# Group normalisation in a ring of six slots: VectorE's loop rewritten with fixed addresses

## Chip, cores and metric

One core of one Trainium2 chip. The metric is the device time of one execution in microseconds (us), median of several runs. The kernel before takes 631.02 us (six runs, 630.43 to 631.61).

## The reference, cut to what matters

```python
# x: [128, 1024, 32, 16] bf16, 32 groups of 32 channels; g, b: [1024] bf16
xr  = x.reshape(B, G, C // G, H, W)
mu  = xr.mean(axis=(2, 3, 4), keepdims=True)
var = ((xr - mu) ** 2).mean(axis=(2, 3, 4), keepdims=True)
xn  = (xr - mu) / jnp.sqrt(var + 1e-5)
return xn.reshape(B, C, H, W) * g[None, :, None, None] + b[None, :, None, None]
```

Every element is read once and written once: 134.22 MB in and 134.22 MB out.

## The kernel before

The 128 images are cut into 32 tiles of 4 images x 32 groups = 128 partitions, each with 16384 elements (4.19 MB). A ring in SBUF has six slots of one tile. For a tile, TensorE adds 12 chunks of 512 columns in PSUM and VectorE adds the rest ("the pair"); ScalarE turns that into the mean, takes the sum of squares in two passes and the standard deviation; VectorE makes scale and bias and applies them in place, one channel (512 columns) per instruction, 32 per tile. Every tile is loaded and stored by one transfer, except that the last one is stored in four parts.

```python
SLOTS = 6
RUNS = (2, 3, 3, 3, 3, 3, 3, 3, 3, 6)       # stores in a row, then as many loads
...
def on_sync(e):                              # issues all transfers, in one queue
    def load(j):
        if j >= SLOTS:
            e.wait_ge(st[j % SLOTS], 16 * (j // SLOTS))       # the slot's store has landed
        e.dma_start(out=slot(j), in_=x_v[j]).then_inc(ld[j % SLOTS], 16)
    def store(i): ...                        # waits for done (VectorE's apply), then dma_start
    for j in range(1, SLOTS):
        load(j)
    i = 0
    for run in RUNS:
        for n in range(run):
            store(i + n)
        i += run
        for j in range(i + SLOTS - run, min(i + SLOTS, NT)):
            load(j)
...
def on_vector(e):
    bytes_of_ring = ring[:].bitcast(mybir.dt.uint8)
    def part(i, lo, n):                      # address from the loop's register
        at = (i % SLOTS) * (F * ITEM) + lo * ITEM
        return bytes_of_ring[:, bass.ds(at, n * ITEM)].bitcast(BF16)
    def pair(i):
        e.wait_ge(first_in, i + 1)           # TensorE's first chunk of this tile
        e.scalar_tensor_tensor(out=jp[:], in0=part(i, lo, n), ..., accum_out=ps[...]).then_inc(paired, 1)
    pair(0)
    with nc.Fori(0, NT, 1, engines=[e.engine]) as i:          # one tile per trip
        with e.If(i < NT - 1):
            e.drain()
            pair(i + 1)
        parts = [part(i, k * HW, HW) for k in range(KC)]
        e.wait_ge(stded, i + 1)
        e.reciprocal(out=rstd[:], in_=std[:, bass.ds(i % SLOTS, 1)]).then_inc(inverted, 1)
        ...                                  # scl, then bia, each after a wait on the one before
        for k, a in enumerate(parts):        # the apply
            ts = e.tensor_scalar(out=a, in0=a, scalar1=scl[:, k : k + 1], scalar2=bia[:, k : k + 1], ...)
            if (k + 1) % KQ == 0:
                ts.then_inc(done, 1)
```

TensorE and ScalarE already loop over six slots with fixed addresses (`in_rounds`: six rounds, of which the last has two tiles).

## Time and profile before

| | before |
|---|---|
| time, median of six | 631.02 us |
| span of the profiled run | 629.3 us |
| busy: VectorE (DVE), ScalarE (ACT), TensorE (PE) | 84%, 80%, 25% |
| mean rate of the transfers | 427 GB/s, in most slices 433 |
| mean granted TensorE clock | 0.595 |

A busy share is an average over stages, so 84% for VectorE says neither that it bounds the kernel nor that it doesn't.

### The profile page before, as it was taken

The page shows a single profiled execution, that of the slowest core. Times are in us where ns is not written, and L with a number is a line of the kernel's source. Part 1 is how long each engine was busy: PE and PEld are TensorE (multiplying, and loading weights), DVE is VectorE, ACT ScalarE, POOL GpSimd, SP SyncE. Part 2 cuts the span into 40 slices and gives each one's busy share as a digit, 9 for nine tenths or more (in the row PEclk, how much of TensorE's full clock was granted, in tenths as well). Part 3 has the DMA queues.
Part 4 walks back from the last instruction along what each step waited for, and adds up shares of the span by engine and source line. Part 5 has one row for each costly group of instructions (what it writes and reads, how often), then busy time and mean ns, then how long its engine had stood idle before and what let it go on. Part 6 is the DMA issues. An engine that isn't in the chain of part 4 may idle for free.

```text
span 629.3 us, 2573 instructions
## 1 busy us (share of the span) xinstructions
PE 157.9 (25%) x380; PEld 0.2 (0%) x2; DVE 529.7 (84%) x1185; ACT 504.0 (80%) x258; POOL 1.0 (0%) x8
## 2 busy tenths in 40 slices
PE   2433333222222220332063014203220430052000
PEld 0000000000000000000000000000000000000000
DVE  1579999999999999699689959995998699599963
ACT  0798999999999999699948977894999489859960
POOL 0000000000000000000000000000000000000000
PEclk9756655566666665566566557656665665576555
DMA  9999999999999999999999999999999999999996
GB/s 400 433 433 402 433 433 433 433 433 431 431 433 433 433 433 433 433 429 433 433 433 431 431 433 431 433 433 433 429 433 433 433 429 433 433 429 431 433 423 271
DMA packets 9744, 268.44 MB, mean 427 GB/s; under 512 B 1168, under 2 KB 1168, under 8 KB 1168
## 3 DMA queue, kind: packets, MB, share of 16 engines
q1 hardware_dynamic: 9648, 268.44, 99.3%
q10 hardware_dynamic: 96, 0.00, 0.0%
HBM read 134.22 MB, written 134.22 MB: 427 GB/s over the span
## 4 chain that ended last, share of the span: by engine, by line
DMA 49%; ACT 35%; DVE 7%; issue 4%; DVEq 2%; PE 2%; SPq 0%; ACTq 0%
DMA out_dram<-ring 33%; ACT ja L259 32%; DMA ring<-in_x_dram 14%; DVE ring L322 6%; DMA gb_b<-in_b_dram 2%; PE ps L213 2%; ACT jm L251 1%; DVEq L305 1%; ACT var L269 1%; ACT std L273 1%; DVE jp L289 0%; DVEq L308 0%; DVE bia L316 0%; DVE scl L312 0%; SPq L158 0%
## 5 line engine op out<-in xcount | busy, mean ns | idle before, releaser
L259 ACT ACTIVATE ja<-ring,nm 128x8192 fp8e5<-128x8192 bf16 x64 | 455.8, 7122 | 2.1
L322 DVE TENSOR_SCALAR ring<-ring,scl,bia x1024 | 333.7, 410 | 1.2
L213 PE MATMUL ps<-ring,eye 128*128 128x512 bf16 x379 | 157.7, 588 | 421.6 <-DVE jp L289 292.3
L289 DVE SCALAR_TENSOR_TENSOR jp<-ring 128x5120 fp8e5 (+1 forms) x32 | 175.8, 5493 | 58.3 <-PE ps L213 46.3
L251 ACT ACTIVATE jm<-ps 128x513 fp8e5<-128x513 f32 x32 | 19.2, 601 | 97.8 <-PE ps L213 97.8
L310 DVE RECIPROCAL rstd<-std 128x1 f32 x32 | 6.3, 198 | 12.1 <-ACT std L273 12.1
L259 ACT ACTIVATION_READ_ACCUMULATOR ja<-ring,nm 128x1 f32 x64 | 11.9, 186 | 0.0
L316 DVE SCALAR_TENSOR_TENSOR bia<-scl,nm,gb 128x32 f32<-128x32 f32 x32 | 8.0, 251 | 4.2
L301 DVE COPY gb<-gb_p 128x64 f32<-128x64 f32 x1 | 0.2, 225 | 12.6 <-PE gb_p L208 12.6
L273 ACT ACTIVATE std<-sq,var 128x1 f32<-128x1 f32 x32 | 9.4, 294 | 1.0
L269 ACT ACTIVATE var<-sq,eps_t 128x1 f32<-128x1 f32 x32 | 9.4, 294 | 1.0
L312 DVE TENSOR_SCALAR scl<-gb,rstd 128x32 f32<-128x32 f32 x32 | 7.7, 241 | 1.1
L251 ACT ACTIVATION_READ_ACCUMULATOR jm<-ps 128x1 f32 x32 | 6.2, 194 | 0.0
L289 DVE DVE_READ_ACCUMULATOR jp<-ring (+1 forms) x32 | 4.5, 142 | 0.0
L208 PE MATMUL gb_p<-gb_b,rep 32*128 32x64 bf16 x1 | 0.2, 206 | 12.4 <-DMA gb_b<-in_b_dram 12.4
L247 ACT ACT_TABLE_LOAD x1 | 1.3, 1283 | 1.8 <-issue 1.8
L190 POOL TENSOR_SCALAR_AFFINE_SELECT rep<-ones_b 32x128 bf16<-32x128 bf16 x1 | 0.3, 302 | 0.0
L186 POOL TENSOR_SCALAR_AFFINE_SELECT eye<-ones_b 128x128 bf16<-128x128 bf16 x1 | 0.3, 292 | 0.4 <-issue 0.4
L247 ACT ACTIVATE warm<-eps_t 128x1 f32<-128x1 f32 x1 | 0.2, 203 | 0.0
L180 POOL MEMSET ones_b<- 128x128 bf16 x1 | 0.2, 204 | 0.3 <-POOLq L355 0.3
L210 PEld LDWEIGHTS <-eye 128*128 128x128 bf16 x1 | 0.1, 106 | 0.1
L208 PEld LDWEIGHTS gb_p<-gb_b,rep 32*128 32x128 bf16 x1 | 0.1, 100 | 12.3 <-issue 12.3
(5 smaller groups left out, 0.5 us busy)
## 6 DMA issues: line engine op xcount, KB each, us to landing
ring<-in_x_dram SPq DMA_DIRECT2D x32, 4096.0 KB, 29.2
out_dram<-ring SPq DMA_DIRECT2D x31, 4096.0 KB, 31.6
out_dram<-ring SPq DMA_DIRECT2D x4, 1024.0 KB, 6.9
gb_b<-in_g_dram ACTq DMA_DIRECT2D x1, 2.0 KB, 7.8
gb_b<-in_b_dram ACTq DMA_DIRECT2D x1, 2.0 KB, 11.0
```

The lines of the kernel that those rows point to most:

```text
L213: return e.add_instruction(mybir.InstMatmult(name=nc.get_next_instruction_name(), engine=e.engine, start_tensor_calc=(k == 0), stop_tensor ...
L247: e.activation(out=warm[:], in_=eps_t[:], func=ACT.Sqrt)
L251: e.activation(out=jm[:], in_=sums_and_pairs(c), func=ACT.Identity, scale=-inv_n, accum_out=nm[:, c : c + 1], saturate=False,).then_inc(me ...
L259: e.activation(out=ja[:], in_=slot(c)[:, h * (F // 2) : (h + 1) * (F // 2)], func=ACT.Square, bias=nm[:, c : c + 1], scale=1.0, accum_out= ...
L269: e.activation(out=var[:], in_=sq[:, 0:1], func=ACT.Identity, bias=eps_t[:], scale=inv_n).then_inc(varred[c], 1)
L273: e.activation(out=std[:, c : c + 1], in_=sq[:, 1:2], func=ACT.Sqrt, bias=var[:], scale=inv_n).then_inc(stded, 1)
L289: e.scalar_tensor_tensor(out=jp[:], in0=part(i, lo, n), scalar=1.0, in1=part(i, lo + n, n), op0=ALU.mult, op1=ALU.add, accum_out=ps[:, bas ...
L305: e.drain()
L310: e.reciprocal(out=rstd[:], in_=std[:, bass.ds(i % SLOTS, 1)]).then_inc(inverted, 1)
L312: e.tensor_scalar(out=scl[:], in0=gb[:, 0:KC], scalar1=rstd[:], scalar2=None, op0=ALU.mult).then_inc(scaled, 1)
L316: e.scalar_tensor_tensor(out=bia[:], in0=scl[:], scalar=nm[:, bass.ds(i % SLOTS, 1)], in1=gb[:, KC : 2 * KC], op0=ALU.mult, op1=ALU.add,). ...
L322: ts = e.tensor_scalar(out=a, in0=a, scalar1=scl[:, k : k + 1], scalar2=bia[:, k : k + 1], op0=ALU.mult, op1=ALU.add,)
```

## The change

VectorE gets the six-slot loop of the other engines. The intent: addresses known when the program is built, no register arithmetic, no drain, semaphores per slot, and less time of VectorE between instructions. A pair now waits for the load itself. Its code becomes some six times as long.

```diff
-            e.wait_ge(first_in, i + 1)
+            e.wait_ge(ld[c], turn * 16)
             e.scalar_tensor_tensor(
                 out=jp[:],
-                in0=part(i, lo, n),
+                in0=slot(c)[:, first : first + w],
 ...
-        with nc.Fori(0, NT, 1, engines=[e.engine]) as i:
-            with e.If(i < NT - 1):
-                e.drain()
-                pair(i + 1)
-            parts = [part(i, k * HW, HW) for k in range(KC)]
-            e.keepalive_nop([e.lower_ap(a) for a in parts])
-            e.wait_ge(stded, i + 1)
-            e.reciprocal(out=rstd[:], in_=std[:, bass.ds(i % SLOTS, 1)]).then_inc(inverted, 1)
+        def one(c, t):
+            then = (c + 1) % SLOTS, t + (1 + (c + 1) // SLOTS)
+            if c == REST - 1:
+                with e.If(t < ROUNDS - 1):
+                    pair(*then)
+            else:
+                pair(*then)
+            e.wait_ge(stded[c], t + 1)
+            e.reciprocal(out=rstd[:], in_=std[:, c : c + 1]).then_inc(inverted[c], 1)
 ...
-            for k, a in enumerate(parts):
+            for k in range(KC):
+                a = slot(c)[:, k * HW : (k + 1) * HW]
 ...
+        pair(0, 1)
+        e.wait_ge(paired[0], 1)
+        in_rounds(e, one)
```

Cut: the semaphores that become one per slot (`paired`, `stded`, `inverted`, `scaled`, `shifted`), TensorE's last chunk waiting on `paired[c]`, and a count of store parts in the load's wait that changes no value here. RUNS and the 12 chunks stay as they were.

More of the change, by code (lines that the diff above doesn't have):

```diff
@@ L128, in sems @@
         return [sem(f"{name}{c}") for c in range(SLOTS)]
-    ld, st, summed, meaned = (sems(n) for n in ("ld", "st", "sum", "mean"))
-    half, both, varred = (sems(n) for n in ("half", "both", "var"))
-    inverted, scaled, shifted = (sem(n) for n in ("inv", "scl", "bia"))
-    first_in, paired, stded, done = (sem(n) for n in ("first", "pair", "std", "done"))
-    s_gb, s_ones, s_eye, s_gbp, s_fin = (
-        sem(n) for n in ("gbl", "ones", "eye", "gbp", "fin")
-    )
+    ld, st, summed, paired, meaned, stded = (
+        sems(n) for n in ("ld", "st", "sum", "pair", "mean", "std")
+    )
+    half, both, varred, inverted, scaled, shifted = (
+        sems(n) for n in ("half", "both", "var", "inv", "scl", "bia")
+    )
+    done = sem("done")
+    s_gb, s_ones, s_eye, s_gbp, s_fin = (sem(n) for n in ("gbl", "ones", "eye", "gbp", "fin"))
     def store_parts(i):
@@ L156, in load @@
             if j >= SLOTS:
-                e.wait_ge(st[j % SLOTS], 16 * (j // SLOTS))
+                e.wait_ge(
+                    st[j % SLOTS], 16 * sum(store_parts(i) for i in range(j % SLOTS, j, SLOTS))
+                )
             e.dma_start(out=slot(j), in_=x_v[j]).then_inc(ld[j % SLOTS], 16)
@@ L234, in one @@
                 elif k == PE_CHUNKS - 1:
-                    e.wait_ge(paired, t * SLOTS + (c + 1))
+                    e.wait_ge(paired[c], t + 1)
                 mm = add_up(sums(c), slot(c)[:, k * MM_FREE : (k + 1) * MM_FREE], k)
-                if k == 0:
-                    mm.then_inc(first_in, 1)
             mm.then_inc(summed[c], 1)
@@ L254, in one @@
             ).then_inc(meaned[c], 1)
-            for h, (ready, at) in enumerate(
-                ((meaned[c], t + (2 if c >= SLOTS - 2 else 1)), (half[c], t + 1))
-            ):
-                e.wait_ge(ready, at)
+            e.wait_ge(meaned[c], t + (2 if c >= SLOTS - 2 else 1))
+            for h in range(2):
+                if h == 1:
+                    e.wait_ge(half[c], t + 1)
                 e.activation(
@@ L266, in one @@
                     saturate=False,
-                ).then_inc((half, both)[h][c], 1)
+                ).then_inc(both[c] if h == 1 else half[c], 1)
             e.wait_ge(both[c], t + 1)
@@ L274, in one @@
                 out=std[:, c : c + 1], in_=sq[:, 1:2], func=ACT.Sqrt, bias=var[:], scale=inv_n
-            ).then_inc(stded, 1)
+            ).then_inc(stded[c], 1)
         in_rounds(e, one)
     def on_vector(e):
-        bytes_of_ring = ring[:].bitcast(mybir.dt.uint8)
-        def part(i, lo, n):
-            at = (i % SLOTS) * (F * ITEM) + lo * ITEM
-            return bytes_of_ring[:, bass.ds(at, n * ITEM)].bitcast(BF16)
-        def pair(i):
-            lo, n = PE_CHUNKS * MM_FREE, PAIRED // 2
-            e.wait_ge(first_in, i + 1)
+        e.wait_ge(s_gbp, 1)
@@ L289, in pair @@
+        e.tensor_copy(out=gb[:], in_=gb_p[:])
+        def pair(c, turn):
+            first, w = PE_CHUNKS * MM_FREE, PAIRED // 2
+            e.wait_ge(ld[c], turn * 16)
             e.scalar_tensor_tensor(
                 out=jp[:],
-                in0=part(i, lo, n),
+                in0=slot(c)[:, first : first + w],
                 scalar=1.0,
-                in1=part(i, lo + n, n),
+                in1=slot(c)[:, first + w : first + 2 * w],
                 op0=ALU.mult,
                 op1=ALU.add,
-                accum_out=ps[:, bass.ds((i % PS_BUFS) * (2 * MM_FREE) + MM_FREE, 1)],
+                accum_out=ps[:, c % PS_BUFS * 2 * MM_FREE + MM_FREE :][:, 0:1],
@@ L297, in pair @@
                 saturate=False,
-            ).then_inc(paired, 1)
-        e.wait_ge(s_gbp, 1)
-        e.tensor_copy(out=gb[:], in_=gb_p[:])
-        pair(0)
-        with nc.Fori(0, NT, 1, engines=[e.engine]) as i:
-            with e.If(i < NT - 1):
-                e.drain()
-                pair(i + 1)
-            parts = [part(i, k * HW, HW) for k in range(KC)]
-            e.keepalive_nop([e.lower_ap(a) for a in parts])
-            e.wait_ge(stded, i + 1)
-            e.reciprocal(out=rstd[:], in_=std[:, bass.ds(i % SLOTS, 1)]).then_inc(inverted, 1)
-            e.wait_ge(inverted, i + 1)
+            ).then_inc(paired[c], 1)
@@ L312, in on_vector @@
+        def one(c, t):
[7 more added lines that the diff above has]
+            e.reciprocal(out=rstd[:], in_=std[:, c : c + 1]).then_inc(inverted[c], 1)
+            e.wait_ge(inverted[c], t + 1)
             e.tensor_scalar(
                 out=scl[:], in0=gb[:, 0:KC], scalar1=rstd[:], scalar2=None, op0=ALU.mult
-            ).then_inc(scaled, 1)
@@ L315, in on_vector @@
-            e.wait_ge(scaled, i + 1)
+            ).then_inc(scaled[c], 1)
+            e.wait_ge(scaled[c], t + 1)
             e.scalar_tensor_tensor(
-                out=bia[:], in0=scl[:], scalar=nm[:, bass.ds(i % SLOTS, 1)],
-                in1=gb[:, KC : 2 * KC], op0=ALU.mult, op1=ALU.add,
-            ).then_inc(shifted, 1)
-            e.wait_ge(shifted, i + 1)
-            for k, a in enumerate(parts):
+                out=bia[:], in0=scl[:], scalar=nm[:, c : c + 1], in1=gb[:, KC : 2 * KC],
+                op0=ALU.mult, op1=ALU.add,
+            ).then_inc(shifted[c], 1)
@@ L322, in on_vector @@
+            e.wait_ge(shifted[c], t + 1)
+            for k in range(KC):
+                a = slot(c)[:, k * HW : (k + 1) * HW]
                 ts = e.tensor_scalar(
```

## The prediction

> **What bounds the kernel now.** I read the strip of DMA share and GB/s first, because a kernel that reads and writes every byte once can be limited by the transfers alone.
>
> ```profile
> DMA  9999999999999999999999999999999999999996
> GB/s 400 433 433 402 433 433 433 433 433 431 431 433 433 433 433 433 433 429 433 433 433 431 431 433 431 433 433 433 429 433 433 433 429 433 433 429 431 433 423 271
> ...
> HBM read 134.22 MB, written 134.22 MB: 427 GB/s over the span
> ```
>
> One slice is 629.3/40 = 15.73 us. The reader is to see a plateau: 433 GB/s in slice after slice, and never more. It is already there in slices 1 and 2, where only loads run, and it stays when loads and stores mix, so it looks like a ceiling of the transfers and not the pace of the compute. At it the 268.44 MB need 268.44/0.433 = 620.0 us. The span is 629.3 us, so 9.3 us are all that any change can win without changing the traffic. Where they are: slice 0 (400) lost 1.2 us at the start, slice 3 (402) lost 1.1 us where the first store comes in, the last slice (271) lost 5.9 us; the rest is slices at 423 to 431.
>
> Next, the chain of work that ended last. It gives ACT 35% and DMA 49%, which looks like a compute limit, but where two things are equally late the chain chooses one. So I checked the compute rhythm against the DMA rhythm. The timeline of VectorE, one tile late in the run:
>
> ```profile
> 492.45 5.49 DVE L289 SCALAR_TENSOR_TENSOR jp<-ring 128x5120 fp8e5 x1 [7.24 <-PE ps L213]
> 497.87 0.14 DVE L289 DVE_READ_ACCUMULATOR jp<-ring  x1
> 497.87 0.20 DVE L310 RECIPROCAL rstd<-std 128x1 f32 x1
> 498.10 0.24 DVE L312 TENSOR_SCALAR scl<-gb,rstd 128x32 f32<-128x32 f32 x1
> 498.48 0.25 DVE L316 SCALAR_TENSOR_TENSOR bia<-scl,nm,gb 128x32 f32<-128x32 f32 x1
> 498.76 10.43 DVE L322 TENSOR_SCALAR ring<-ring,scl,bia  x32
> 509.69 5.49 DVE L289 SCALAR_TENSOR_TENSOR jp<-ring 128x5120 fp8e5 x1 [0.50 <-issue]
> ```
>
> Two things are to be seen. From pair to pair is 509.69 - 492.45 = 17.24 us, the pace of compute when it isn't waiting. A tile moves 8.39 MB, 19.4 us at 433 GB/s, so compute is 2.1 us per tile faster than DMA. And the first line: VectorE waited 7.24 us for a tile to arrive (TensorE's first chunk, itself waiting for the load). It does so about once per run of three.
>
> Third, the waits of the DMA-issuing queue and the time to landing:
>
> ```profile
> SPq L164 <- DVE ring L322: 366.1, 28, 43.3
> SPq L158 <- DMA out_dram<-ring: 227.4, 25, 11.7
> ...
> ring<-in_x_dram SPq DMA_DIRECT2D x32, 4096.0 KB, 29.2
> out_dram<-ring SPq DMA_DIRECT2D x31, 4096.0 KB, 31.6
> ```
>
> The issuing queue waits 366.1 us for VectorE, which would suggest that a faster VectorE pays. The last two lines contradict it: a 4.19 MB transfer alone takes 9.7 us at 433 GB/s, yet 29 to 32 us pass from issue to landing. So about 20 us of other transfers lie ahead of each one. Issuing earlier only lengthens that queue.
>
> [...] The trace has 10.43/32 = 326 ns[...]. [...] I count some 38 instructions per tile in the new loop, about 230 for six tiles[...]. [...]
>
> **The change part by part.** The few words name runs of three and 12 chunks, but neither constant is touched by the diff: TensorE and ScalarE do the same work in the same order, and the order of transfers is the same. Only VectorE's control changes, plus which semaphores carry it.
>
> 1. The drain and the register arithmetic ahead of each pair go. The 0.50 us before the pair (24 such gaps, 12.0 us in the waits) should shrink to the 0.03 us seen between other neighbours: about 0.47 us per tile.
> 2. The register operation between scl and bia goes. scl starts at 498.10 and bia at 498.48, 0.14 us after scl's 0.24 are over; reciprocal to scl has a gap of 0.03. About 0.10 us per tile.
> 3. The pair waits for the load itself rather than for TensorE's first chunk. Where the tile is late, TensorE starts at 550.27 and the pair only at 551.22: about 0.95 us, some eight to ten times in the run.
> 4. The apply (32 x 326 ns), the pair (5.49 us) and ScalarE's two 7.12 us passes stay, as data and operators stay.
>
> So the compute pace becomes 17.24 - 0.57 = 16.67 us. ScalarE and TensorE do not allow much less: ScalarE's sequence took 122.17 to 138.00 = 15.83 us in another tile, plus 0.62 us for the last TensorE chunk, 16.45. Summed over 32 tiles this is 32 x 0.57 + 9 x 0.95 = 26.8 us of VectorE time. Nearly all lies beside the transfers: compute was already 2.1 us per tile ahead, and now is 2.7 ahead. VectorE will only wait longer for loads, which cannot come sooner.
>
> **The end, the one place where it could count.** The last load was issued at 540.6 and landed near 570; from there compute drains alone. The pair of the third last tile starts at 551.22 and the last apply ends at 619.2. Savings on that path: 0.95 (step 3) + 2 x 0.57 + 0.10 = 2.2 us, so the last store part would be issued near 617.0. The DMA share around there, in windows:
>
> ```profile
> 600.00:610.00 10.00, 0.00 (x0) 0.00 (x0) 4.34 (x15) 7.71 (x4) 0.00 (x0) 0.50 0.98 423
> 610.00:619.20 9.20, 0.00 (x0) 0.00 (x0) 9.20 (x29) 0.00 (x0) 0.00 (x0) 0.50 0.96 405
> 619.20:623.30 4.10, 0.00 (x0) 0.00 (x0) 0.00 (x1) 0.00 (x0) 0.00 (x0) 0.50 0.95 396
> 623.30:629.30 6.00, 0.00 (x0) 0.00 (x0) 0.00 (x0) 0.00 (x0) 0.00 (x0) 0.50 0.13 53
> ```
>
> The last two columns are DMA share and GB/s. While VectorE writes its last tile the transfers still run at 0.95 to 0.98, so they are not waiting for it, or hardly. Then from 623.3 the share is 0.13: a few of the 16 engines are behind the rest and finish some 5 us later. My choice is that these late engines set the end: they had work all the time, so an earlier last store does not move them, and the others only become idle sooner. I put the win at a fifth of 2.2 us, about 0.4 us: 631.04 - 0.4 = 630.6.
>
> **Rivals.**
> - The end follows VectorE after all: if the late engines were waiting for the last part as well, all 2.2 us come off and the time is 628.8. For it: the chain ends in VectorE's apply and a store. Against it: the share of 0.95 and more until 623.3.
> - [...]
> - Instruction fetch: the VectorE code grows from one tile to six, and each return to the loop's top might stall. A round of six tiles has 6 x 2.7 = 16 us of slack, so only longer stalls would show in the middle; at the last return, ahead of the last two tiles, some 4 us can hide. A stall of 10 us there would give about 636. Against it: ScalarE and TensorE go round their six-tile loops with no gap beyond the usual.
> - The DMA rhythm gets worse because stores come in a little earlier against loads. The order in the queue is fixed by the issuing program, and 20 us wait in it, so I expect nothing: 631.
>
> **Range and chances.** Before repeats within 630.43 to 631.47. The mechanism in the middle allows no change; the end allows up to 2.2 us less, a stall a little more. Predicted 630.6, range 628.8 to 632.0. Faster by 2% means below 618.4, under the 620.0 that the bytes take at the plateau: 0.01. Slower by 2% means above 643.7, some 13 us of new stall at the end: 0.02. Within 2%: 0.97.
>
> **What would show it.** Right: the GB/s strip stays at 433 with about the same first and last slices; VectorE's pair-to-pair distance without a wait is near 16.7 us and the 0.50 us "issue" gap is gone; VectorE's waits for loads grow by more than 20 us; the last apply ends near 617 and the span still ends 628 to 630. Wrong: the span ends 2 us sooner together with the last apply (first rival); the apply's spacing is no longer 326 ns (second); VectorE shows idle time attributed to issue at every sixth tile (third); the plateau leaves 433 (fourth). The prediction as a whole would be wrong if the 433 GB/s were itself paced by VectorE, which the load-only slices speak against.

The 0.4 (a fifth of 2.2) is my estimate from the savings and DMA shares above. Cut is what no trace or run here shows: where the 433 GB/s come from, how the apply's 326 ns come about and how much code VectorE holds, and with them the second rival, in which fixed addresses make the apply faster; its test, the apply's spacing, stays. Where the third rival says that ScalarE and TensorE go round with no gap beyond the usual, the waits of the kernel before have 1.1 us on issue for TensorE's matmuls, in five gaps of at most 0.2 us, and none for ScalarE inside its loop.

## The result, and the profile after

| | before | after |
|---|---|---|
| time, median of six | 631.02 us | 631.91 us (631.70 to 632.47) |
| ratio | | 1.0014 (1.0002 to 1.0027) |
| span of the profiled run | 629.3 us | 630.1 us |
| VectorE from pair to pair, not waiting | 17.24 us | 16.55 us |
| end of the last apply | 619.20 us | 617.73 us |

A ratio here is the mean time of one kernel's fast runs over that of the other's of the same rounds, so it is not quite the ratio of the medians; the bracket is a 95% interval.

The page of the kernel after, its strips of DMA share and GB/s and its DMA queues (packets, MB, share of 16 engines):

```profile
DMA  9999999999999999999999999999999999999995
GB/s 400 433 433 399 433 435 429 433 433 433 433 439 435 433 433 435 433 429 433 433 433 433 433 435 431 433 431 433 429 433 433 435 424 433 433 429 439 433 421 251
...
q1 hardware_dynamic: 9648, 268.44, 99.2%
q10 hardware_dynamic: 96, 0.00, 0.0%
q14 instruction: 2, 0.02, 0.0%
```

The plateau (slices of 421 to 439, most at 433), the first slice (400) and the dip at the first store (399, before 402) are as they were. The last slice fell from 271 to 251. The last line is new: two packets of an instruction queue. The kernel before has none inside its span.

VectorE's timeline around a tile late in the run (start, duration, what):

```profile
509.50 5.49 DVE L288 SCALAR_TENSOR_TENSOR jp<-ring 128x5120 fp8e5<-128x5120 bf16 x1
514.91 0.14 DVE L288 DVE_READ_ACCUMULATOR jp<-ring 128x1 f32 x1
514.91 0.20 DVE L308 RECIPROCAL rstd<-std 128x1 f32<-128x1 f32 x1
515.15 0.24 DVE L310 TENSOR_SCALAR scl<-gb,rstd 128x32 f32<-128x32 f32 x1
515.43 0.25 DVE L314 SCALAR_TENSOR_TENSOR bia<-scl,nm,gb 128x32 f32<-128x32 f32 x1
515.71 10.42 DVE L321 TENSOR_SCALAR ring<-ring,scl,bia 128x512 bf16<-128x512 bf16 x32
526.05 5.49 DVE L288 SCALAR_TENSOR_TENSOR jp<-ring 128x5120 fp8e5<-128x5120 bf16 x1
```

526.05 - 509.50 = 16.55 us, where it was 17.24. The 0.50 us ahead of the pair are gone (the apply ends at 526.13 by its record, and the pair already starts), and bia follows scl after 0.28 us, not 0.38. The apply takes 10.42 us for 32 instructions as before (10.43), so the fixed addresses made it no faster.

The waits of the kernel after (total us, times, longest):

```profile
DVE jp L288 <- DMA ring<-in_x_dram: 60.5, 8, 8.9
DVE rstd L308 <- ACT std L275: 12.7, 2, 7.3
...
SPq L168 <- DVE ring L321: 340.6, 26, 42.9
SPq L162 <- DMA out_dram<-ring: 251.9, 26, 12.7
```

VectorE's waits for loads grew from 46.3 us (then attributed to TensorE's first chunk) to 60.5, and the wait on issue (12.0 us before) is no longer there. The issuing queue shows the same exchange: it waits 25.5 us less for VectorE (366.1 to 340.6) and 24.5 us more for stores to land (227.4 to 251.9). The saving became waiting.

Last, the windows at the end of the kernel after (the last two columns are DMA share and GB/s):

```profile
600.00:610.00 10.00, 0.00 (x0) 0.00 (x0) 4.53 (x16) 6.45 (x4) 0.00 (x0) 0.50 0.98 423
610.00:619.20 9.20, 0.00 (x0) 0.00 (x0) 7.73 (x24) 0.00 (x0) 0.00 (x0) 0.50 0.98 419
619.20:623.30 4.10, 0.00 (x0) 0.00 (x0) 0.00 (x0) 0.00 (x0) 0.00 (x0) 0.50 0.86 362
623.30:629.30 6.00, 0.00 (x0) 0.00 (x0) 0.00 (x0) 0.00 (x0) 0.00 (x0) 0.50 0.18 78
```

Between 619.2 and 623.3 the share fell from 0.95 to 0.86, as the last parts were issued 1.5 us sooner and most DMA engines ran dry sooner; after 623.3 it rose from 0.13 to 0.18. The engines that are behind were further behind.

**How far behind.** Each transfer reports 16 completions (1072 packets of 4 B for 67 transfers); I take them as one per DMA engine, as the packets form 16 chains, each packet starting where another ends. From these records of the trace I took, for single transfers, the time from the first to the last of the 16 ("spread"). The records don't name the engine. The transfers are those that landed near 40, 90 and 150 us, and the store of tile 30, the last whole one. All times in us, from each kernel's profiled run:

| kernel | fetch packets at | spread near 40 | near 90 | near 150 | tile 30's store: first of 16 | its spread | span |
|---|---|---|---|---|---|---|---|
| before | none | 0.49 | 0.65 | 1.04 | 603.2 | 5.60 | 629.3 |
| after | 46.9, 106.2 | 0.46 | 2.26 | 4.02 | 603.3 | 6.50 | 630.1 |
| e1 | none | 0.49 | 0.62 | 0.64 | 603.2 | 3.79 | 627.1 |
| e2 | 50.5, 107.5 | 0.57 | 2.14 | 2.93 | 603.2 | 5.85 | 629.3 |
| e3 | none | 0.42 | 0.49 | 0.72 | 603.4 | 4.97 | 628.7 |
| e5 | 47.8, 107.0 | 0.54 | 1.47 | 2.59 | 603.1 | 5.82 | 629.2 |
| e7 | 27.5, 33.3 (and 624.7) | 2.28 | 3.27 | 3.25 | 603.1 | 6.74 | 630.9 |
| e8 (after) | 46.8, 106.5 | 0.57 | 1.85 | 2.84 | 603.4 | 5.84 | 629.5 |
| e12 (after) | 46.8, 106.2 | 0.42 | 1.90 | 3.92 | 603.4 | 6.66 | 630.4 |

Two things are to be seen. The first engine lands tile 30 at 603.1 to 603.4 in every one of these kernels, with much compute, little, or none; the span is this plus the spread plus about 20 us (20.1 to 21.1). So the latest of the 16 DMA engines sets the end. And in every kernel of the table with fetch packets at about 47 and 106 us the spread grows by 0.8 to 2.0 us from the column ahead of each to the one behind it, where kernels without them grow by 0.4 us or less. (e6 has both fetches too and is left out, as its VectorE is slower: tile 30 first lands at 604.7, with a spread of 5.35.)

**What a fetch does.** The kept traces also have each packet's start and length. The packets of one engine follow each other within some 10 ns, so each fetch can be placed on an engine. In the kernel after, the fetch at 46.92 takes 0.325 us between two data packets of one engine, and the next data packet there takes 1.88 us, not the usual 1.21. The fetch at 106.21 lies on the same engine: 0.31 us, then a packet of 1.56. Together they cost this engine 1.65 us. Besides, a data packet there took 2.42 us at 58.8, where the first store comes in and the others have packets of up to 1.9, and one took 2.24 us at 99.1 without a recorded fetch, so part of the growth from 40 to 90 us, and 1.03 us of that from 90 to 150, are not shown to be a fetch's. e12 has one of 2.42 us at 98.9; e2, e5 and e8 have none above 1.6 us near 99, and they end with the smaller spreads (5.82 to 5.85, against 6.50 and 6.66).

Not all of this lasts: near 150 us the spread is 3.0 us above that of the kernel before, at tile 30 only 0.9, as in the kernel before an engine falls behind later without any fetch (1.04 to 5.60).

### The profile page after: what moved, and what is told of

The parts are those of the page before. It is cut to its first block, busy times and chain, and to the rows that moved or that the text cites. A ratio compares the mean times of both kernels' runs of the same rounds, so it can differ in the third digit from the quotient of the medians.

```text
span 630.1 us, 2036 instructions
## 1 busy us (share of the span) xinstructions
PE 157.6 (25%) x380; PEld 0.2 (0%) x2; DVE 528.4 (84%) x1185; ACT 504.0 (80%) x258; POOL 1.0 (0%) x8
## 4 chain that ended last, share of the span: by engine, by line
DMA 63%; DVE 29%; ACT 5%; issue 1%; PE 0%; SPq 0%; DVEq 0%; ACTq 0%
DMA out_dram<-ring 43%; DMA ring<-in_x_dram 18%; DVE ring L321 18%; DVE jp L288 10%; ACT ja L261 5%; DMA gb_b<-in_b_dram 2%; DVE bia L314 0%; DVE scl L310 0%; ACT jm L253 0%; SPq L162 0%; PE ps L217 0%; DVE rstd L308 0%; ACT var L271 0%; ACT std L275 0%; DVEq L369 0%
## 5 line engine op out<-in xcount | busy, mean ns | idle before, releaser
L321 DVE TENSOR_SCALAR ring<-ring,scl,bia 128x512 bf16<-128x512 bf16 x1024 | 333.5, 406 | 1.2
L288 DVE SCALAR_TENSOR_TENSOR jp<-ring 128x5120 fp8e5<-128x5120 bf16 x32 | 175.5, 5485 | 60.5 <-DMA ring<-in_x_dram 60.5
L308 DVE RECIPROCAL rstd<-std 128x1 f32<-128x1 f32 x32 | 5.7, 179 | 12.7 <-ACT std L275 12.7
L288 DVE DVE_READ_ACCUMULATOR jp<-ring 128x1 f32 x32 | 4.5, 140 | 0.0
```

The lines of the kernel that those rows point to most:

```text
L288: e.scalar_tensor_tensor(out=jp[:], in0=slot(c)[:, first : first + w], scalar=1.0, in1=slot(c)[:, first + w : first + 2 * w], op0=ALU.mult ...
L308: e.reciprocal(out=rstd[:], in_=std[:, c : c + 1]).then_inc(inverted[c], 1)
```

## The experiments

Two questions: why 0.69 us per tile on the busiest engine gave nothing, and where the 0.9 us came from. For the second, theory A is the two instruction fetches, theory B the new rhythm of stores and loads. e1 to e4 ran on one chip, e5 to e8 on a second, e9 to e12 on a third, each beside the kernel before, and only ratios and differences to that are compared.

### e1: the transfers alone

```diff
-        (TensorE, ScalarE, GpSimd and VectorE as in the changed kernel)
+        def one(c, t):
+            e.wait_ge(ld[c], (t + 1) * 16)
+            e.drain()
+            for q in range(NQ):
+                e.memset(scl[:, q : q + 1], 0.0).then_inc(done, 1)
```

> Wrong result on purpose: no compute at all, VectorE only answers each landed load with four tiny memsets, so the same loads and stores go out in the same order (the output is the input). Theory (the transfers set the time, and the late DMA engines set the end): 628 to 631.5 us, GB/s strip at 433, and the spread between the first and the last of the 16 engines to land the last transfers still 4 to 6 us. Rival (compute paces part of the run, or the end follows the last apply): at least 3 us faster than the kernel before, below 628 us, with a spread under 1.5 us at the end.

Measured: 629.38 us (four runs, 628.28 to 630.13) against 630.72, ratio 0.9977 (0.9961 to 0.9992). Its output is wrong, which doesn't matter for the time. The strip of GB/s:

```profile
GB/s 401 435 435 401 435 435 435 435 435 435 433 433 433 433 433 433 431 433 431 433 431 428 435 435 426 435 435 435 435 431 433 435 428 433 433 435 431 435 433 301
```

Removing all compute wins 1.3 us. The first slice and the dip in the fourth stay (401 each), so both belong to the transfers. The spread at the end is 3.79 us, a little under the expected 4 to 6, but far from the rival's 1.5. With this order of transfers, no change to VectorE should win more than about this (0.5 to 2.5 us by the interval).

### e2: the changed kernel with the drain back

```diff
             first, w = PE_CHUNKS * MM_FREE, PAIRED // 2
+            e.drain()
             e.wait_ge(ld[c], turn * 16)
```

> The changed kernel with the drain put back ahead of each pair, so VectorE has its old pace of about 17.1 us per tile but keeps the long code and its two instruction fetches. Theory A (the 0.9 us lost come from the two fetches that delay one DMA engine): 631.9 us like the changed kernel, two fetch packets on the instruction queue. Theory B (the 0.9 us come from the changed rhythm, stores issued sooner among the loads): back to 631.0 us like the kernel before.

Measured: 631.05 us, ratio 1.0007 (0.9993 to 1.0021), two fetch packets. By its time it looks like theory B, but the premise fell: the pace was 16.74 us (pairs at 508.79 and 525.53), not 17.1. With fixed addresses the drain costs 16.74 - 16.55 = 0.19 us. So the rhythm was hardly restored, and the interval holds both 1.0000 and 1.0014: this run doesn't tell the theories apart.

### e3: the kernel before without the drain

```diff
             with e.If(i < NT - 1):
-                e.drain()
                 pair(i + 1)
```

> The kernel before without the drain: VectorE gets most of the new pace (about 16.8 us per tile), the code stays short. Theory A (fetches): no fetch packet inside the run and 631.0 us like the kernel before. Theory B (rhythm): 631.9 us like the changed kernel. Both: VectorE's 0.50 us gap ahead of the pair shrinks, no gain of over 1 us.

Measured: 631.04 us, ratio 1.0005 (0.9991 to 1.0018), correct, no fetch packet. VectorE's timeline:

```profile
508.95 5.50 DVE L289 SCALAR_TENSOR_TENSOR jp<-ring 128x5120 fp8e5 x1
...
514.61 0.24 DVE L311 TENSOR_SCALAR scl<-gb,rstd 128x32 f32<-128x32 f32 x1
514.98 0.25 DVE L315 SCALAR_TENSOR_TENSOR bia<-scl,nm,gb 128x32 f32<-128x32 f32 x1
515.27 10.43 DVE L321 TENSOR_SCALAR ring<-ring,scl,bia  x32
525.61 5.49 DVE L289 SCALAR_TENSOR_TENSOR jp<-ring 128x5120 fp8e5 x1
```

The pace is 16.66 us (508.95 to 525.61), almost that of the changed kernel, with code for one tile and register addresses. So nearly the whole saving can be had by removing the drain. The packed trace of the kernel before also has the drain and the register instructions: ahead of the pair at 509.69 the drain lasts from 505.75 to 509.24, past the apply's end at 509.19, and the pair's register instructions follow from 509.28 to 509.64. Those of the apply (L308), behind no drain, run from 509.75 to 510.50 beside the pair. That in e3 the pair's run beside the apply in the same way is my reading, not measured. Drain alone costs 0.19 us (e2), register work alone 16.66 - 16.55 = 0.11 us (the gap ahead of bia, which e3 keeps: scl at 514.61, bia at 514.98), both together 0.69. The fast rhythm without fetches isn't measurably slower than the kernel before. That speaks against B, but weakly, as the interval holds B's 1.0014 too.

### e4: a block that is never executed, once per round

```diff
+        def one_and_skip(c, t):
+            one(c, t)
+            if c == 0:
+                with e.If((t * t) % 7 == 5):        # never true
+                    for _ in range(640):
+                        e.memset(var[:], 0.0)
```

> The changed kernel with a block of 640 instructions inside the loop that is never executed, jumped over once per round (six times)[...]. Theory A: [...]the time rises by 10 us or more and the spread at the end grows well past 6.5 us. Theory B: fetches are harmless to the transfers: under 633 us, whatever their number, as VectorE has 2.7 us of slack per tile to hide its own stalls.

Its "10 us or more" leaned on that count and on 1.8 us per fetch, the growth of the spread in the kernel after (0.46 to 2.26 and 2.26 to 4.02); without the count it is only my guess.

Measured: 656.96 us, ratio 1.0426 (1.0409 to 1.0443), correct. Its page, strips and the instruction queue:

```profile
DMA  9999999999999999999999999999999999999583
GB/s 387 447 419 414 447 421 443 427 438 424 435 431 435 431 432 431 428 429 437 435 427 441 423 428 435 393 415 407 427 416 384 421 441 363 431 427 399 235 364 165
...
q14 instruction: 34, 0.28, 0.1%
```

34 packets of 8192 B took about 0.32 us each, and 26.2 us were lost: 0.77 us of the kernel's time per fetch. How that comes about is in its waits:

```profile
DVE jp L288 <- DMA ring<-in_x_dram: 64.8, 8, 10.8
DVE jp L288 <- issue: 17.8, 7, 3.2
```

VectorE itself stalls 17.8 us ahead of pairs at the jumps, at most 3.2 at a time. The records of completion show the other side: the transfer that landed near 380 us has a spread of 19.15 us, with 15 of its 16 completions within 2.5 us and one far behind. This one engine is late, every transfer waits for it, and as only some 21 to 25 us of transfers are queued (30.3 us from issue to landing for a load and 34.3 for a store, less 9.7 for itself), the others then wait too. The packets give the cost: in all 34 cases the next data packet of the fetch's engine takes 1.67 to 1.88 us in place of 1.21, so that with the fetch itself 30.4 us are lost on the engine (0.89 per fetch), beside the 26.2 us of the kernel. Theory A holds for many fetches.

### e5 and e6: a little more work on VectorE

```diff
             e.wait_ge(inverted[c], t + 1)
+            e.memset(jp[:, 0:1440], 0.0)            # e6: 0:4800
```

> The changed kernel with one more VectorE instruction per tile, a memset of 1440 elements, about 1.5 us by the pair's 5.49 us per 5120 elements. Theory (VectorE has some 2.7 us of slack per tile): pace 16.6 + 1.6 = 18.2 us, below the 19.4 us of the transfers, so the time stays at 631 to 633 us although VectorE works about 50 us more. Rival (VectorE's time counts): up to 50 us more, 680 us.

> The same with 4800 elements, about 5.1 us per tile: pace 21.7 us, above the 19.4 us of the transfers. Theory: VectorE now sets the time; pair 2 starts near 51 us, pair 31 near 51 + 29 x 21.7 = 680, then 5.6 + 17 + 15.5 us to the last apply's end and 4 us for the last store, about 722 us (715 to 730), with GB/s below 433 in the strip. If the slack were much larger than thought, the time would stay under 650 us.

Measured: e5 631.13 us, ratio 1.0007 (0.9992 to 1.0022); e6 631.88 us, ratio 1.0014 (0.9999 to 1.0030). Both sizes were wrong, from my error: the memset was issued packed, as the group shows for e6:

```profile
L310 DVE MEMSET jp<- 128x1200 uint32 x32 | 33.9, 1058 | 10.1 <-DVE rstd L308 10.1
```

1200 words in 1.06 us, not 4800 elements in 5.1. The pace in e6 was 17.68 us (510.42 to 528.10), almost wholly hidden: the ratio's interval still holds 1, but the last apply ended at 621.2, 2.0 us later than in the kernel before. The intended test had to be repeated.

### e9 and e10: the same, sized by a known operation

```diff
             e.wait_ge(inverted[c], t + 1)
+            e.scalar_tensor_tensor(
+                out=jp[:, 0:2240], in0=slot(c)[:, 0:2240], scalar=1.0, in1=slot(c)[:, 2240:4480],
+                op0=ALU.mult, op1=ALU.add, saturate=False,
+            )                                       # e10: 5120
```

> The memset of the last two runs turned out to be packed (1.1 us in place of 5), so this uses the pair's own operation on 2240 elements, 2.4 us by the pair's 5.49 us per 5120. Pace 16.6 + 2.5 = 19.1 us per tile, still below the 19.4 us of the transfers. First theory (slack counted per tile, as in the prediction): unchanged, under 633 us. Second theory (slack counted over the whole run, with the 48 us before pair 2 and about 38 us after pair 31 that are not overlapped): 48 + 29 x 19.1 = 602 for pair 31, + 37 to the end of the last apply, + 6, about 645 us; the break-even pace would then be 18.5 us, not 19.4.

> The same with 5120 elements, 5.5 us: pace 22.1 to 22.2 us, slower than the transfers under both ways of counting. VectorE sets the time: pair 2 near 51.5 us, pair 31 near 51.5 + 29 x 22.15 = 694, last apply's end near 732, in all 733 to 743 us. If it stays under 700, VectorE's time is hidden in a way that neither theory knows.

Measured: e9 640.92 us, ratio 1.0162 (1.0146 to 1.0177); e10 733.70 us, ratio 1.1632 (1.1615 to 1.1650). The strip of e9, and its waits for loads, which were 60.5 us in the kernel after:

```profile
GB/s 394 431 433 415 427 441 433 277 394 429 425 427 427 433 443 437 427 427 431 433 439 435 427 431 431 435 437 433 425 437 431 439 423 435 431 435 433 433 277 361
```

```profile
DVE jp L288 <- DMA ring<-in_x_dram: 3.7, 1, 3.7
```

The time of e9 lies between its two expectations, under 633 and about 645, and rules out the first. At a pace of 18.95 us (484.19 to 503.14) VectorE waits for one load only, and the strip has holes (277 in the eighth slice and near the end), although 18.95 is below the 19.4 us that a tile's bytes need. Slack per tile is thus not 19.4 minus the pace. A better count is from pair 2 to pair 31, which took 585.71 - 46.98 = 538.7 us in the kernel before, 18.58 us per tile: the first loads run without stores and the last stores without loads. Against this, e9 is 0.37 us per tile too slow, 29 x 0.37 = 10.7 us; 10.2 were measured. For e10 (pace 21.95) it is 29 x 3.37 = 97.7 plus one more 5.5 us operation ahead of the last apply, 103.2; 103.0 were measured. That both sums come so close is in part luck. In the traces the last apply ends 14.4 us later than in the kernel before (e9) and 107.6 us later (e10), and the span ends only 9.6 and 102.8 us later, since the tail behind the last apply is 5.3 us in both and was 10.1. So 18.58 us is an estimate of the pace that still costs nothing; e6 (17.68, 0.9 us slower by its ratio) and e9 (18.95, 10.2 us) enclose it. By it the slack was 18.58 - 17.24 = 1.34 us per tile before the change and about 2.0 after.

### e7: the never executed block in the kernel before

```diff
+            with e.If((i * i) % 7 == 5):            # never true
+                for _ in range(640):
+                    e.memset(var[:], 0.0)
             parts = [part(i, k * HW, HW) for k in range(KC)]
```

> The kernel before with the never executed block of 640 instructions jumped over once per tile (32 times) in place of once per round. Theory A (each instruction fetch takes time of one DMA engine: 26 us for 34 fetches in the run with one jump per round): 4 to 7 fetches per trip, 130 to 220 packets, 100 us or more above 631, one DMA engine always 20 us behind. Rival (the cost came from VectorE's stalls at the jump, not from the DMA engine): the number of fetches per trip is the same, but the stall per tile must fit into 2.1 us to be hidden; the strip would then show all engines idle together and no growing spread.

(The 4 to 7 fetches per trip are an estimate from e4: 34 fetches over six jumps.)

Measured: 632.69 us, ratio 1.0027 (1.0012 to 1.0043). Its queues:

```profile
q14 instruction: 4, 0.02, 0.0%
```

One of the four is a packet of 40 B at the very start. The dose didn't come: three fetches of 8192 B (27.5, 33.3 and 624.7 us), not 130 or more. With 32 jumps and three fetches, a jump that is taken didn't by itself cost a fetch here; why so few came was not shown. As a test it is better than planned: VectorE's timeline is that of the kernel before (17.24 us per tile, the 0.50 us gap included), and with two early fetches, one late, the time rises by 0.27% and the final spread from 5.60 to 6.74 us. The packets agree: the two early fetches cost one engine 1.93 us, and behind the late one a packet of the last store takes 0.66 us in place of 0.31. Fetches without the new rhythm cost time; the new rhythm without fetches (e3) did not measurably.

### e8 and e12: the changed kernel again

No edit.

> The changed kernel unaltered, once more beside the kernel before. If the 0.9 us are a property of the kernel: a ratio of 1.0014 again (0.5 to 1.3 us slower). If they belong to the one chip or session of the first comparison: a ratio whose interval holds 1.0000, as in the runs with the drain moved.

> The changed kernel a third time beside the kernel before. The first look gave 1.0014 (1.0002 to 1.0027), the second 1.0004 (0.9991 to 1.0018). If the change costs anything, the ratio is above 1 again: 1.0003 to 1.0014, 0.2 to 0.9 us. If not, 0.9995 to 1.0003.

Measured: e8 631.15 us, ratio 1.0004 (0.9991 to 1.0018), an interval that holds 1, as expected for the case that the 0.9 us belong to one chip or session; e12 631.99 us, ratio 1.0021 (1.0007 to 1.0034), above the range. By the means of the three comparisons the changed kernel is 0.9, 0.4 and 1.3 us slower. The spread of tile 30's store orders their profiled runs as their spans do: 5.84, 6.50 and 6.66 us for 629.5, 630.1 and 630.4 us.

### e11: two blocks per round

```diff
-            if c == 0:
+            if c in (0, 3):
                 with e.If((t * t) % 7 == 5):
```

> The changed kernel with two never executed blocks per round in place of one (eleven jumps in all). Theory A (each fetch delays one DMA engine by some 0.77 us, 26.2 us over 34 fetches): 55 to 75 fetch packets and 670 to 690 us, with the last of the 16 engines again about 20 us behind. Rival (a few stalls of VectorE at the wrong place cost the 26 us, not the number of fetches): about 657 to 662 us although there are more fetches.

(The 55 to 75 packets are an estimate from e4: 34 for six jumps, so about 62 for eleven.)

Measured: 668.69 us, ratio 1.0607 (1.0587 to 1.0627), between the two expectations. Its instruction queue and its stalls at the jumps:

```profile
q14 instruction: 45, 0.37, 0.1%
```

```profile
DVE jp L288 <- issue: 16.3, 8, 2.4
```

There were 45 packets, fewer than expected, and 38.0 us lost: 0.84 us per fetch, after 0.77 in e4. VectorE's stalls on issue are no longer than in e4 (16.3 after 17.8 us) while the loss is 11.8 us larger. So the loss follows the number of fetches, not VectorE's stalls; again one engine ran about 20 us behind (spread 21.53 near 380 us).

No version with the right result beat the kernel before: e1 bounds what is to be had at 1.3 us, and e3, which has nearly the whole pace without the fetches, is level with it.

## Why the prediction was right, and where not

**The bound: right.** The 433 GB/s plateau is a limit of the transfers. e1 shows it without any compute (433 to 435 GB/s in most slices, 629.38 us), and e9 and e10 show the other side, where a slower VectorE tears holes into it.

**The parts of the change: right in kind.** The pace fell to 16.55 us, where 16.67 was predicted. Steps 1 and 2 measured 0.69 us together instead of 0.57. What the prediction took for two separate costs ahead of the pair looks like one interaction: 0.19 us for a drain alone, 0.11 for register work alone, 0.69 for both (e2, e3), and in the kernel before the register work ahead of the pair starts only behind the drain (509.28, after its end at 509.24).

**Step 3 fell.** The pair of the third last tile was to start 0.95 us sooner. It started at 551.35, before at 551.22: it did follow the load at once, but that load landed at 551.32 instead of 550.23, because of the late engine. So the last apply ended 1.5 us sooner, not 2.2. VectorE's waits for loads grew by 14.2 us, not by more than 20: the sum of 26.8 us counted 32 gaps ahead of the pair where the trace has 24 (12.0 us), and 8.55 us of step 3 that did not come.

**The slack: mis-sized.** "2.1 us ahead per tile" compared the pace with the bytes of one tile; over the run it was about 1.3 us (an estimate; e6, e9 and e10). It didn't matter here, since the change made VectorE faster.

**The end: the mechanism right, the sign of the rest wrong.** The prediction chose that late DMA engines set the end and an earlier last store does not move it. That holds: the last apply came 1.5 us sooner, and the span ended 0.8 us later. The term that failed is "a fifth of 2.2 us, about 0.4 us": measured were +0.9 us. It left out that the change itself could make an engine later. That 631.91 still lies in the range, 0.1 us below its upper end of 632.0, is luck: the range reached up for a stall of VectorE, and none came.

**The instruction-fetch rival: the wrong place.** The prediction looked for a stall of VectorE and took the code, some 230 instructions, to be small enough. VectorE has no gap on issue in the kernel after. But two fetches came, and each made one of the DMA engines later; in the kernel after this engine stays the latest to the end, by 1.3 us or more from 90 us on. That fetches do this is shown packet by packet, with many (e4, e11) and with few in the old rhythm (e7). That all of the 0.9 us is theirs is the best reading but not settled: three comparisons gave 0.4 to 1.3 us, and e2 and e5, with the same two fetches, gave ratios of 1.0007 whose intervals include 1, no more than e3's 1.0005 without a fetch.

Open: why DMA engines drift behind without any fetch (5.60 us in the kernel before, 3.79 with no compute), which engines these are, and what the long packets at 99 us are in the kernel after and e12. Part of the drift comes in steps: in the kernel before, from 61 us on, all data packets of over 1.4 us (usual: 1.21) start near 157, 215, 273, 331, 390, 448, 506 and 565 us, about every 58 us, where a run of loads gives way to a run of stores.

## What to carry to other kernels

Before speeding up an engine, compare the byte count over the plateau rate with the span (here 620.0 and 629.3 us), and see how long the transfers queue. Here about 20 us of transfers lay ahead of each new one, and the faster VectorE only waited longer: 60.5 us for loads, where it was 46.3. Count the slack of an engine over the whole run, first tile and last included, not per tile (here about 1.3 us, an estimate, and not 2.1). With the transfers at 433 GB/s, even fetching instructions took from them: unrolled loops with jumps cost here 0.77 us per fetch with 34 fetches (e4) and 0.84 with 45 (e11).
